# Linear attention into a two-layer expert on one core: the divided rows stored from GpSimd's queue, SyncE's transfers of a slot in another order, early fetches of late operands, weight sums loaded a period ahead

## The chip, the cores and the metric

One core of one Trainium2 chip runs the whole program. The metric is the device time of one execution in microseconds, as the median of several runs. Engines: PE (TensorE matmul), PEld (its weight loads), DVE (VectorE), ACT (ScalarE), POOL (GpSimd), SP (SyncE, which here only issues DMA transfers). SP and POOL each issue their transfers in the order of their program. An instruction that waits holds back all that stands behind it on its engine, transfers too.

## The reference

Random-feature linear attention for 8 batches and 8 heads (576 rows of 64), and then one expert (512 to 2048 to 512) with a leaky rectifier over all 4608 rows:

```python
def phi(x):
    proj = np.einsum('bhsd,df->bhsf', x, w_phi)
    proj = proj - np.max(np.abs(proj), axis=-1, keepdims=True)
    return np.concatenate([np.exp(proj), np.exp(-proj)], axis=-1)
q_p, k_p = (phi(q), phi(k))
kv = np.einsum('bhsf,bhsd->bhfd', k_p, v)
z = np.sum(k_p, axis=2)
num = np.einsum('bhsf,bhfd->bhsd', q_p, kv)
den = np.einsum('bhsf,bhf->bhs', q_p, z)[..., None] + 1e-06
attn = num / den
# x = attn as (4608, 512)
h = x @ w_in
g = np.maximum(h, 0.0) + alpha * np.minimum(h, 0.0)
out = g @ w_out
```

## The kernel before

**Attention.** The work is cut into 32 units, one for each batch and pair of heads. `places(i)` gives each step of a unit a due time, counted in slots from the unit's number, and the steps of all units are sorted by these times; so a slot holds steps of four neighbouring units. In this first part the order on PE, SP, DVE and ACT is the sorted order, and POOL's order is the scheduler's. PE projects q and k (`pj`, `pl`, L330) from `raw` (loaded at L291), DVE takes the maxima (L334) and subtracts them (L335), ACT takes exponentials, PE sums `kv` (L372, L389), then the denominators `d` (L455) and the numerators `n` (L437).

**The division** goes through DRAM to turn rows into another layout. ACT copies the denominators to `ds` (L465), SP sends 4.5 KB of them back as a tile of 128 rows of 9 (`den_out`, L469), DVE takes the reciprocal (`invert`, L474), SP writes it to `rec_d` (`rec_out`, L477) and reads it back twice as a broadcast over 64 partitions (`spread`, `rr`, L482), POOL multiplies the numerators `s` with it (`finish`, L487), and SP stores the result to `x_d` (`store`, L490). The transfers of a slot are 576 KB for `raw`, 320 for `v`, 512 for `raww`, 512 for `u_d` or `v_d`, 256 for `a_d`, twice 144 for `rr`, 288 for `x_d`, and 4.5 each for `d` and `rec_d`.

**Weights.** Once a slot a block of the weights, which arrive as pairs of 32-bit words, is decoded by the times of the table `W`: SP loads `raww` (L165), ACT, DVE (L182 to L190) and POOL (L194) put a 32-bit float together, ACT casts its high part (L133), POOL subtracts for the low part (L137), and SP stores the float to `a_d` (L214) and the two parts to `u_d` or `v_d` (L215).

**The expert** keeps each product in three matmuls (high by high, low by high, high by low). The first 512 rows are done plainly: `up2` (tile `h`, L528 to L530) and `down2` (`po`, L537 to L539), 4 products of each in an order unit of about 2.8 us. Their operands are `xr0` (the first 512 rows, 1 MB, L564), `wo` (weights of the first up products, six of 512 KB, L604) and `wd` (of the down products, 1 MB each, L597). The other 4096 rows go in four pairs of 512-row chunks by a scheme with 7 products in place of 8: eight units of up products (7 products of 6 matmuls, L803 to L805, out tiles `pa`, `pb`, `pc`), then the down products (`qa`, `qb`, `qc`) with weights `wv` that SP loads at L898.

**Sums of weights.** The 7-product scheme needs sums of weight blocks. For each of 8 up and 8 down units `sums` has five steps: `load` (POOL's queue, `a_d` to `su` or `sv`, L661), `two` (DVE, L670 and L671), `four` (DVE, L676 and L677), `high` (ACT cast, L133), and `rest` (DVE low part, L137, and two stores from POOL's queue to `us_d` or `vs_d`, L688). The table `SUMS` places the first ten of them; the other six (`v2` to `v7`) go one to a unit in the first pair's loop.

**Rows for the pairs.** `prepare(p)` loads two tiles `xr` of 1 MB each from `x_d` (POOL's queue, L743; one buffer) and makes seven operands `xo` of each on ACT (L133) and DVE (L137, L750).

In this second part the order on PE, SP and POOL is that of the program, and DVE and ACT are ordered by the scheduler. The sums of the first pair's loop live in a pool `sq` of four buffers. It is closed before the seventh unit of the pair, and the pool of `wv` takes its place, so that the first `wv` load has to wait for the last stores out of `sq`.

Of the kernel before, what the change touches and what calls it, by code (L numbers as in the profile page):

```python
# [8 lines left out]
F32 = mybir.dt.float32  # L9
# [7 lines left out]
P = 128  # L17
# [24 lines left out]
RW_BUFS = 4  # L42
# [16 lines left out]
def places(i):  # L59
    early = i < ZP  # L60
    end = i >= NPAIR - 2
    first = {}
    if i == 0:
        first = dict(
            kz=0.5093, ka=0.6934, ko=0.8124, kr=1.1197, kc=1.4241,
            n=1.8361, q=(0.96, 0.9362, 0.4904), qe=(0.9994, 1.4139, 0.8939),
        )
    if i == 1:
        first = dict(kz=0.0015, ka=0.0046, ko=0.0058)
    return dict(  # L70
        ld=-1.9685,
        lv=-0.6051,
        p=(-0.9955 if early else -0.997, -0.2197),
        pl=-0.2217,
        ke=(-0.1643, -0.0202),
        ks=(-0.0999, 0.2674, 0.4111),
        kz=0.9861,
        ka=1.0012,
        ko=1.0028,
        kr=1.0191,  # L80
        kc=1.1461,
        q=(1.4089, 1.4543, 1.3558),
        qe=(1.4364, 1.4627, 1.3892),
        d=1.9966,
        ds=2.0026,
        n=2.0062,
        s=2.1311,
        d9=2.3091,
        dv=2.7686 if early else 2.842 if end else 2.7432,
        rd=2.9461 if early else 3.1211 if end else 2.8029,  # L90
        rr=3.2683 if early else 3.3511 if end else 2.967,
        x=3.3998 if early else 3.4169 if end else 3.0674,
        xs=3.7743 if early else 3.7643 if end else 3.402,
    ) | first


W = dict(load=-0.6044, scale=-0.2534, split=-0.1196, rest=0.0025, add=0.4009, high=0.635, low=0.7532, store=0.999)
X0T = (27.2, 28.2, 28.7, 29.2, 29.7)
X0L = 0.1151
WDT = (27.5, 28.5)  # L100
WUT = (28.0, 28.4, 28.8)
HEADS = (31.9, 32.3, 32.62, 32.9)
T2 = 33.05
HEAD = 4
# [1 line left out]
U2 = 1 / 3  # L106
GQ = (0.1093, 0.2682, 0.3222)
UPA = 2
SUM0, SUMD = 2.0, 2.6
SUMS = (0.0, 0.9, 1.3, 1.7, 2.5)  # L110
NDS = 2
XP0, XPD = 8.0, 1.45


@with_exitstack
def fused_kernel(ctx: ExitStack, tc: tile.TileContext, kq, v, w_phi, w_in, w_out, alpha, out):
# [116 lines left out]
    def behind(eng):  # L233
        return tc.issue_after(newest[eng].ins)
# [49 lines left out]
    def attention_units(i):  # L284
# [202 lines left out]
            pool.tensor_tensor(c["s"], c["s"], c["r"], op=ALU.mult)  # L487

        def store():
            nc.sync.dma_start(x_d[hp, :, b * S : (b + 1) * S], c["s"])  # L490

        at = places(i)
        us = [
# [156 lines left out]
    def sums(u, down=False):  # L650
        k = "v" if down else "u"
        st = {}

        def load():
            if "sq" in late:
                tiles = [late["sq"].tile([P, 4 * WN], F32, tag="sq", name=f"s{k}_{u}_{n}", bufs=4) for n in range(3)]
            else:
                tiles = [late["s"].tile([P, 4 * WN], F32, tag="s", name=f"s{k}_{u}", bufs=3)]
                tiles += [w1t.tile([P, 4 * WN], F32, tag="wraw", name=f"sd{k}_{u}_{n}", bufs=RW_BUFS) for n in range(2)]
            a = tiles[0].rearrange("p (n c) -> p n c", n=4)  # L660
            pool.dma_start(a, a_d[int(down), u])  # L661
            a11, a12, a21, a22 = (a[:, n] for n in ((0, 2, 1, 3) if down else (A11, A12, A21, A22)))
            src = (a[:, 0:2], a[:, 2:4]) if down else (a[:, 1:3], a[:, 0:4:3])
            dst = [t.bitcast(F32R).rearrange("p (n t c) -> p n t c", t=2, c=WN) for t in tiles[1:]]
            st.update(pairs=list(zip((0, 2), src, dst)), b=(a11, a12, a21, a22))

        def two():
            a11, a12, a21, a22 = st["b"]
            with behind("dve"):
                dve.tensor_tensor(a22, a21, a22, op=ALU.add)  # L670
                dve.tensor_tensor(a21, a11, a21, op=ALU.subtract)  # L671

        def four():
            a11, a12, a21, a22 = st["b"]
            with behind("dve"):
                dve.tensor_tensor(a11, a22, a11, op=ALU.subtract)  # L676
                dve.tensor_tensor(a12, a12, a11, op=ALU.subtract)  # L677

        def high():
            with behind("act"):  # L680
                for n, a, t in st["pairs"]:
                    rnd(act, t[:, :, 0], a)

        def rest():
            for n, a, t in st["pairs"]:
                with behind("dve"):
                    low(dve, t[:, :, 1], a, t[:, :, 0])
                pool.dma_start((us_d, vs_d)[down][u, :, n : n + 2], f(t))  # L688

        return load, two, four, high, rest  # L690
# [98 lines left out]
        for dt, g in zip(SUMS, parts):  # L789
            todo.append((t1 + (SUM0 + SUMD * n + dt) * U2 + 0.002, g))  # L790
    for n in range(16):
        todo.append((t1 + (XP0 + XPD * n) * U2 + 0.003, lambda n=n: (prep.extend(prepare(1) if n == 0 else []), pieces(1))))
    end = t1 + (len(order) - HEAD) * U2 - 0.002
    todo.append((end, lambda: load_up(1, 0)))
    todo.append((end + 10, turn_on))
# [178 lines left out]
    with tc.manual_schedule(engines={et.PE, et.SP, et.Pool}):  # L974
# [10 lines left out]
        for p in range(1, NC2 // 2 + 1):  # L985
            more_pairs = p < NC2 // 2
            queue += [(p, k, u) for k in range(len(ORDER)) for u in range(NU)]
            for u in range(NU):
                if p == 1 and u == NU - 2:
                    sq.close()  # L990
                    late["wv"] = ctx.enter_context(tc.tile_pool(name="wvp", bufs=4, reuse_waits="tile"))
                if u == UX and more_pairs:
                    prep += prepare(p + 1)
                    pieces(1)
                if u == NU - 1:
                    for h in range(3):
                        load_wv(p, 0, h)
                if p == 1 and u == 0:
                    vs = [sums(n, True) for n in range(NDS, NU)]
                    vs[0][0]()  # L1000
                if p == 1 and u < len(vs):
                    for g in vs[u][1:]:
                        g()
                    if u + 1 < len(vs):
                        vs[u + 1][0]()
                if u or p > 1:
                    ahead[1]()
                if u + 1 < NU:
                    load_up(p, u + 1)
                if u == 0 and p == 1:  # L1010
                    for h in held:
                        give(*h)
                ahead[2]()
                now, ahead = ahead, unit(p, u + 1) if u + 1 < NU else None
                if ahead:
                    ahead[0]()
                else:
                    for _ in range(NLAST):
                        next(downs)
                now[3]()  # L1020
                if u < NH - 1:
                    some_operand()
                if u == NU - 2:
                    downs = down_pair(p)
            some_operand()
            if more_pairs:
                load_up(p + 1, 0)
                ahead = unit(p + 1, 0)
            for n, _ in enumerate(downs):
                if more_pairs and n == len(ORDER) * NU * 2 - NLAST - NNEXT:  # L1030
                    ahead[0]()
# [39 lines left out]
```

## Time and profile before

| what | value |
|---|---|
| median of 3 runs | 1160.08 us (1158.88, 1160.08, 1166.88) |
| the profiled execution's own time, and its span | 1160.64 us, 1158.8 us |
| PE busy | 1064.1 us, 92% of the span |
| PEld, DVE, ACT busy | 824.5, 751.7, 615.4 us |
| POOL busy | 176.5 us |
| moved by DMA | 270.11 MB, mean 233 GB/s |
| chain that ended last | PE 76%, DMA 10%, issue 8%, DVE 3%, POOL 2% |

Times in the rows are microseconds from the start of the span. In a row of the timeline the first number is the start, the second the duration, then engine, line, operation and `out<-in`; square brackets hold the idle time of the engine just before, and what ended it. Attention runs from about 20 to 385 us, the first 512 rows to 457 us, and the four pairs from there to the end.

### The profile page before, as it was taken

The numbers are of one execution on the slowest core, as the hardware profiler recorded it, in microseconds if no ns is written. First come the engines' busy times: TensorE is split into PE (matmuls) and PEld (weight loads), VectorE is DVE, ScalarE is ACT, GpSimd is POOL, SyncE is SP. The second block draws the span as 40 slices with busy tenths as digits, with TensorE's granted clock in tenths as the row PEclk, the third lists the DMA queues.
The fourth block names the chain that finished last, engine by engine and source line by source line (L and its number), as shares of the span: only waits on it lengthen the run. The fifth ranks groups of instructions, "written<-read, shape, count | busy, mean of one in ns | idle before, by whom it ended". The sixth has DMA issues, their size and how long they took to land.

```text
span 1158.8 us, 19845 instructions
## 1 busy us (share of the span) xinstructions
PE 1064.1 (92%) x7601; PEld 824.5 (71%) x7601; DVE 751.7 (65%) x1205; ACT 615.4 (53%) x1164; POOL 176.5 (15%) x192
## 2 busy tenths in 40 slices
PE   9999999999879998299609999999999999999998
PEld 6676666667556786278408888888788887888887
DVE  7868777677654345558628665588745696555764
ACT  5777777677556323245405554465544565444553
POOL 1334333333323210111110010000100001000000
PEclk9999999999999999599859999999999999999999
DMA  5888897887995697587657766566755757555465
GB/s 186 267 254 266 249 268 244 258 267 251 303 319 166 187 358 295 200 294 273 241 183 243 240 208 215 191 237 198 265 208 191 245 181 254 191 189 194 161 205 177
DMA packets 107582, 270.11 MB, mean 233 GB/s; under 512 B 18848, under 2 KB 19488, under 8 KB 106464
## 3 DMA queue, kind: packets, MB, share of 16 engines
q1 hardware_dynamic: 95632, 227.09, 60.1%
q0 software_dynamic: 11568, 41.69, 9.9%
q8 instruction: 60, 0.98, 0.3%
q14 instruction: 34, 0.28, 0.1%
q10 hardware_dynamic: 288, 0.07, 0.0%
HBM read 207.69 MB, written 60.96 MB: 232 GB/s over the span
## 4 chain that ended last, share of the span: by engine, by line
PE 76%; DMA 10%; issue 8%; DVE 3%; POOL 2%; ACT 1%; SPq 1%; ACTq 0%; POOLq 0%; DVEq 0%
PE kv L372 5%; PE n L437 5%; PE pa L803 5%; PE pa L804 5%; PE pa L805 5%; PE pj L330 5%; PE qa L803 4%; PE qa L804 4%; PE qa L805 4%; PE kv L389 3%; PE qc L803 3%; PE qc L805 3%; PE qc L804 3%; PE pc L805 2%; PE pc L804 2%
## 5 line engine op out<-in xcount | busy, mean ns | idle before, releaser
L137 DVE TENSOR_TENSOR hv<-g,hv 128x512 fp32r<-128x512 f32 x224 | 152.5, 689 | 79.1 <-ACT hv L133 78.9
L133 ACT CAST hv<-g 128x512 fp32r<-128x512 f32 x224 | 138.6, 622 | 122.0 <-DVE hv L137 55.3
L803 PE MATMUL qa<-hv,wv 128*128 128x512 f32 (+1 forms) x257 | 100.7, 392 | 39.1 <-DMA wv<-v_d 39.1
L804 PE MATMUL qa<-hv,wv 128*128 128x512 f32 (+1 forms) x257 | 100.5, 391 | 0.0
L805 PE MATMUL qa<-hv,wv 128*128 128x512 f32 (+1 forms) x257 | 100.2, 390 | 0.0
L707 POOL DMA_DIRECT2D out_dram<-pt x31 | 17.0, 547 | 531.8 <-ACT pt L970 443.6
L330 PE MATMUL pj<-w_sb,raw 64*128 64x128 f32 x1024 | 74.2, 285 | 17.8 <-issue 12.5
L330 PEld LDWEIGHTS pj<-w_sb,raw 64*128 64x128 f32 x1024 | 65.0, 193 | 30.9 <-issue 22.3
L334 DVE TENSOR_REDUCE m<-pj 128x8 f32<-128x1024 f32 (+2 forms) x67 | 78.4, 1170 | 9.1 <-PE pj L330 9.0
L803 PEld LDWEIGHTS qa<-hv,wv 128*128 128x128 f32 x257 | 48.6, 189 | 49.9 <-DMA wv<-v_d 39.6
L335 DVE TENSOR_TENSOR t<-pj,m 128x1024 f32<-128x1024 f32 (+2 forms) x67 | 78.9, 1177 | 4.8 <-ACT s L448 0.5
L437 PE MATMUL n<-qf,sf 128*64 128x288 f32 x512 | 72.3, 427 | 0.0
L487 POOL TENSOR_TENSOR s<-s,rr 128x576 f32<-128x576 f32 x32 | 45.5, 1422 | 151.8 <-DMA rr<-rec_d 142.0
L349 ACT ACTIVATE xk<-t 128x1024 f32<-128x1024 f32 (+1 forms) x66 | 64.3, 1028 | 4.7 <-DVE t L335 4.7
L428 ACT ACTIVATE qf<-qt 128x512 f32<-128x512 f32 x128 | 66.8, 633 | 0.0
L823 ACT ACTIVATE r<-g 128x512 f32<-128x512 f32 x65 | 37.6, 624 | 50.7 <-DVE g L819 50.7
L372 PE MATMUL kv<-xk,v 128*64 128x256 f32 x512 | 62.3, 385 | 0.0
L824 DVE SCALAR_TENSOR_TENSOR g<-r,al,g 128x512 f32<-128x512 f32 x65 | 46.2, 748 | 18.1 <-ACT r L823 18.1
L474 DVE RECIPROCAL r<-d 128x9 f32<-128x9 f32 x32 | 6.9, 215 | 76.6 <-DMA d<-ds 76.6
L194 POOL TENSOR_TENSOR aw<-ew,aw 128x512 f32<-128x512 f32 x32 | 40.7, 1273 | 101.4 <-DVE ew L190 101.4
L805 PEld LDWEIGHTS qa<-hv,wv 128*128 128x128 f32 x257 | 48.7, 189 | 10.2
L804 PEld LDWEIGHTS qa<-hv,wv 128*128 128x128 f32 x257 | 48.7, 189 | 10.1
(177 smaller groups left out, 2568.3 us busy)
## 6 DMA issues: line engine op xcount, KB each, us to landing
ws<-us_d SPq DMA_DIRECT2D x64, 512.0 KB
wv<-vs_d SPq DMA_DIRECT2D x64, 512.0 KB, 4.3
wv<-v_d SPq DMA_DIRECT2D x48, 512.0 KB, 5.0
wa<-u_d SPq DMA_DIRECT2D x37, 512.0 KB
raw<-kq_dram SPq DMA_DIRECT2D x31, 576.0 KB, 6.0
v<-v_dram SPq DMA_DIRECT2D x32, 320.0 KB, 7.2
rr<-rec_d SPq DMA_DIRECT2D x64, 144.0 KB, 5.8
x_d<-s SPq DMA_DIRECT2D x32, 288.0 KB, 2.3
```

The source lines that it names most:

```text
L133: return act.copy(dst, src)
L137: return eng.tensor_tensor(dst, src, f(hi), op=ALU.subtract)
L330: pe.matmul(dst[h, j], lhsT=c["raw"][hs, ts], rhs=w_sb[hs], start=True, stop=True)
L334: dve.tensor_reduce(m, src, axis=AX.X, op=ALU.max, apply_absolute_value=True)
L335: dve.tensor_tensor(t[:, hs, js], src, m.unsqueeze(3).broadcast_to([P, nh, nj, FD]), op=ALU.subtract)
L349: act.activation(x[:, a, :, js], c["t", 0][:, :, js], AF.Exp, scale=sg)
L372: pe.matmul(c["kv"][h * D : (h + 1) * D, 0:2], lhsT=c["v"][:, tp, h, :], rhs=c["x", ch][:, :, h, j, :], start=tp == 0, stop=tp == NV - 1,)
L428: act.activation(c["qf"][:, h, a, : 4 * P], ps.rearrange("p j f -> p (j f)"), AF.Exp, scale=sg)
L437: pe.matmul(ps[h * D : (h + 1) * D, :], lhsT=c["st"][:, a, h * D : (h + 1) * D], rhs=c["qf"][:, h, a, u * HS : (u + 1) * HS], start=a == 0 ...
L803: pe.matmul(ps, lhsT=wh, rhs=xh, start=first, stop=False, skip_group_check=True)
L804: pe.matmul(ps, lhsT=wl, rhs=xh, start=False, stop=False, skip_group_check=True)
L805: pe.matmul(ps, lhsT=wh, rhs=xl, start=False, stop=end, skip_group_check=True)
```

## The change

The store of the divided rows (`store`) goes from SP's queue to POOL's, where it follows `finish`. The due times of SP's steps in a slot are moved, so that its nine transfers of a slot come in another order. `xr0` is fetched 8 slots earlier, the two `wd` tiles 12.3 and 10.3 slots, the three pairs of `wo` 15.8, 7.2 and 4.6 slots, and the first `xr` of the first pair goes from the stage of the first 512 rows to slot 24.5 of attention. `sums` takes its output tiles in `high` and no longer in `load`, `SUMS` puts `load` 3.0 order units ahead of `two`, and in the first pair's loop the next `load` stands before the stores of the sum at hand. No arithmetic is added or taken out. From L653 on the line numbers rise by 1 to 3 (L661 becomes L662, L688 L690, L743 L745, L819 L822).

```diff
@@ places
-        ld=-1.9685,
-        lv=-0.6051,
+        ld=-1.65,
+        lv=-0.45,
...
-        d9=2.3091,
+        d9=2.025,
...
-        rd=2.9461 if early else 3.1211 if end else 2.8029,
-        rr=3.2683 if early else 3.3511 if end else 2.967,
+        rd=2.82,
+        rr=3.03,
...
-W = dict(load=-0.6044, ..., store=0.999)
-X0T = (27.2, 28.2, 28.7, 29.2, 29.7)
+W = dict(load=-0.83, ..., store=0.9)
+X0T = (19.2, 20.2, 21.2, 22.2, 23.2)
...
-WDT = (27.5, 28.5)
-WUT = (28.0, 28.4, 28.8)
+WDT = (15.2, 18.2)
+WUT = (12.2, 21.2, 24.2)
...
-SUM0, SUMD = 2.0, 2.6
-SUMS = (0.0, 0.9, 1.3, 1.7, 2.5)
+SUM0, SUMD = 3.1, 2.6
+SUMS = (-3.0, 0.0, 0.2, 0.6, 1.0)
...
-XP0, XPD = 8.0, 1.45
+XP0, XPD = 8.0, 1.35
...
         def store():
-            nc.sync.dma_start(x_d[hp, :, b * S : (b + 1) * S], c["s"])
+            pool.dma_start(x_d[hp, :, b * S : (b + 1) * S], c["s"])
...
         def high():
+            dst = [st["new"](n + 1).bitcast(F32R).rearrange("p (n t c) -> p n t c", t=2, c=WN) for n in range(2)]
+            st["pairs"] = list(zip((0, 2), st["src"], dst))
...
     for n in range(16):
-        todo.append((t1 + (XP0 + XPD * n) * U2 + 0.003, lambda n=n: (prep.extend(prepare(1) if n == 0 else []), pieces(1))))
+        t = t1 + (XP0 + XPD * n) * U2 + 0.003 if n else 24.5
+        todo.append((t, lambda n=n: (prep.extend(prepare(1) if n == 0 else []), pieces(1))))
...
                 if p == 1 and u < len(vs):
-                    for g in vs[u][1:]:
+                    for n, g in enumerate(vs[u][1:]):
                         g()
-                    if u + 1 < len(vs):
-                        vs[u + 1][0]()
+                        if n == 2 and u + 1 < len(vs):
+                            vs[u + 1][0]()
```

In `sums.load` the lines that took three tiles now take one, and leave a function `st["new"]` for the other two; up sums now take all three names from one counter (`su_1`, `su_2` in place of `sdu_0`, `sdu_1`).

SP in one slot of attention, before (`s` divided rows, `r` reciprocals, `aw` a decoded float, `raww` its raw words or two parts, `ds` denominators):

```order
L490 DMA x_d<-s_2575 128x576
L477 DMA rec_d<-r_15_2767 128x9
L214 DMA a_d<-aw_0_0_2612 128x512
L215 DMA u_d<-raww_0_0_2585 128x1024
L291 DMA raw_2877<-kq_dram 128x1152
L482 DMA rr_2884<-rec_d 64x576 x2
L469 DMA d_16_2887<-ds_2846 128x1x9
L165 DMA raww_1_0_2889<-w_out_dram 128x1024
L295 DMA v_2898<-v_dram 128x640
```

And in the changed kernel, in the slot that also holds the early `xr0`:

```order
L469 DMA d_17_3037<-ds_3006 128x1x9
L482 DMA rr_3039<-rec_d 64x576 x2
L165 DMA raww_1_0_3042<-w_out_dram 128x1024
L564 DMA xr_3049<-x_d 128x4x512
L291 DMA raw_3051<-kq_dram 128x1152
L295 DMA v_3075<-v_dram 128x640
L477 DMA rec_d<-r_17_3081 128x9
L214 DMA a_d<-aw_1_0_2924 128x512
L215 DMA v_d<-raww_1_0_2888 128x1024
```

The store of `s` is gone from the row, `d` comes first, and `raw` comes behind the broadcast reads and the weight load instead of ahead of them.

POOL's queue at the second `xr` of the first pair (`su` the floats of an up sum, `sdu` or `su_1`, `su_2` its two output tiles), before:

```order
L661 DMA su_5520<-a_d 128x1024
L688 DMA us_d<-sdu_0_5521 128x1024
L688 DMA us_d<-sdu_1_5522 128x1024
L661 DMA su_5583<-a_d 128x1024
L743 DMA xr_1_5630<-x_d 128x2x1024
L688 DMA us_d<-sdu_0_5584 128x1024
```

And in the changed kernel:

```order
L690 DMA us_d<-su_1_5500 128x1024
L690 DMA us_d<-su_2_5501 128x1024
L662 DMA su_5528<-a_d 128x1024
L690 DMA us_d<-su_1_5559 128x1024
L690 DMA us_d<-su_2_5560 128x1024
L662 DMA su_5606<-a_d 128x1024
L745 DMA xr_1_5610<-x_d 128x2x1024
L690 DMA us_d<-su_1_5630 128x1024
```

Before, a load is followed by the stores of the same sum; now a load stands ahead of the stores of the sum before it. In both, `xr_1` comes behind the stores of the sixth sum.

DVE at the end of the up units of the first pair, where `g_7_11` takes PE's last product ahead of the down products (`pa_7`); before:

```order
L137 TENSOR_TENSOR sv_1_5988<-sv_0_5987,sv_1_5988 128x2x256
L819 TENSOR_TENSOR g_7_11_6526<-pa_7_6480,p_1_7_6545 128x512
L137 TENSOR_TENSOR sv_2_5989<-sv_0_5987,sv_2_5989 128x2x256
L137 TENSOR_TENSOR xo_2_0_6732<-xr_0_6069,xo_2_0_6732 128x512
L137 TENSOR_TENSOR xo_3_0_6809<-xr_0_6069,xo_3_0_6809 128x512
...
L137 TENSOR_TENSOR sv_2_6083<-sv_0_6081,sv_2_6083 128x2x256
...
L137 TENSOR_TENSOR sv_2_6175<-sv_0_6173,sv_2_6175 128x2x256
...
L137 TENSOR_TENSOR sv_2_6267<-sv_0_6265,sv_2_6267 128x2x256
```

And in the changed kernel:

```order
L137 TENSOR_TENSOR sv_2_6258<-sv_0_6169,sv_2_6258 128x2x256
L822 TENSOR_TENSOR g_7_11_6526<-pa_7_6480,p_1_7_6545 128x512
L137 TENSOR_TENSOR xo_4_0_6886<-xr_0_6067,xo_4_0_6886 128x512
L670 TENSOR_TENSOR sv_0_6261<-sv_0_6261 128x256
L671 TENSOR_TENSOR sv_0_6261<-sv_0_6261 128x256
L676 TENSOR_TENSOR sv_0_6261<-sv_0_6261 128x256
L677 TENSOR_TENSOR sv_0_6261<-sv_0_6261 128x256
L137 TENSOR_TENSOR sv_1_6347<-sv_0_6261,sv_1_6347 128x2x256
L137 TENSOR_TENSOR sv_2_6348<-sv_0_6261,sv_2_6348 128x2x256
```

Before, three whole sums (`v5`, `v6`, `v7`) stand behind `g_7_11`; now only the last.

## Rows read from the trace of the kernel before

**Rows 1.** The waits of PE, longest first: line, what it waited for, us in total, times, longest.

```profile
PE qa L803 <- DMA wv<-v_d: 39.1, 1, 39.1
PE pa L803 <- ACT xo L133: 26.5, 1, 26.5
PE pj L330 <- issue: 12.5, 5, 3.7
```

**Rows 2.** PE's timeline: the first `kv` row of a slot, the first and the last of 29 (34.82 and 354.42), two neighbours (264.02 and 274.59), and one slot with its first `pj` (140.94 to 154.94).

```profile
34.82 1.95 PE L372 MATMUL kv<-xk,v 128*64 128x256 f32 x16
...
140.94 1.95 PE L372 MATMUL kv<-xk,v 128*64 128x256 f32 x16
...
145.03 1.16 PE L330 MATMUL pj<-w_sb,raw 64*128 64x128 f32 x16 [1.72 <-issue]
...
154.94 1.95 PE L372 MATMUL kv<-xk,v 128*64 128x256 f32 x16
...
264.02 1.95 PE L372 MATMUL kv<-xk,v 128*64 128x256 f32 x16
...
274.59 0.65 PE L372 MATMUL kv<-xk,v 128*64 128x256 f32 x4
...
354.42 1.95 PE L372 MATMUL kv<-xk,v 128*64 128x256 f32 x16
```

**Rows 3.** The waits views of SP's queue, of POOL and of DVE, one row of each, in the same columns as rows 1.

```profile
SPq L490 <- POOL s L487: 146.9, 32, 6.4
...
POOL s L487 <- DMA rr<-rec_d: 142.0, 30, 11.1
...
DVE r L474 <- DMA d<-ds: 76.6, 30, 5.4
```

**Rows 4.** The timelines of ACT, DVE, POOL and SP over the slot from 262.5 to 275, an engine at a time.

```profile
266.51 0.39 ACT L465 ACTIVATE ds<-d 128x288 f32<-128x288 f32 x1
...
273.19 0.22 DVE L474 RECIPROCAL r<-d 128x9 f32<-128x9 f32 x1 [2.94 <-DMA d<-ds]
...
262.46 1.42 POOL L487 TENSOR_TENSOR s<-s,rr 128x576 f32<-128x576 f32 x1 [3.87 <-DMA rr<-rec_d]
263.84 1.29 POOL L137 TENSOR_TENSOR raww<-aw,raww 128x512 fp32r<-128x512 f32 x1
...
273.87 1.42 POOL L487 TENSOR_TENSOR s<-s,rr 128x576 f32<-128x576 f32 x1 [4.72 <-DMA rr<-rec_d]
...
263.91 0.33 SPq L490 DMA_DIRECT2D x_d<-s  x1
...
265.31 0.39 SPq L215 DMA_DIRECT2D v_d<-raww  x1
265.80 0.41 SPq L291 DMA_DIRECT2D raw<-kq_dram  x1
266.54 1.18 SPq L482 DMA_DIRECT2D rr<-rec_d  x2
267.81 0.58 SPq L469 DMA_DIRECT2D d<-ds  x1
```

**Rows 5.** Two landing times: the last line of the view of L291 (the `raw` loads), from issue to landing; and the last broadcast reads of attention on SP's timeline, when little else was in flight.

```profile
DMA to landing us min/median/max: 4.3/5.8/7.9
...
398.60 1.10 SPq L482 DMA_DIRECT2D rr<-rec_d  x2
```

**Rows 6.** A table of stretches: from, to, length, then busy time and instructions of PE, PEld, DVE, ACT and POOL, granted clock, DMA share, GB/s.

```profile
197.00:300.00 103.00, 98.73 (x1301) 69.29 (x1295) 76.09 (x126) 73.95 (x157) 37.99 (x29) 1.00 0.82 258
300.00:360.00 60.00, 48.95 (x592) 34.21 (x590) 37.12 (x59) 36.28 (x82) 15.68 (x12) 0.94 0.90 303
```

**Rows 7.** POOL's timeline in the stage of the first 512 rows: the last `finish`, the first sum's stores, the second `xr`.

```profile
402.39 1.67 POOL L487 TENSOR_TENSOR s<-s,rr 128x576 f32<-128x576 f32 x1 [10.27 <-DMA rr<-rec_d]
404.02 1.13 POOL L688 DMA_DIRECT2D us_d<-sdu  x2
...
475.56 0.71 POOL L743 DMA_DIRECT2D xr<-x_d  x1
```

**Rows 8.** PE's timeline around its first long stop: the last up product's last matmul, the first matmul after the stop; and the view of L743 (`xr`), its last line.

```profile
454.49 0.40 PE L530 MATMUL h<-x0pt,ws 128*128 128x512 f32 x1
...
484.88 0.79 PE L803 MATMUL pa<-xo,wa 128*128 128x512 f32 x1 [26.52 <-ACT xo L133]
...
DMA to landing us min/median/max: 5.8/8.9/11.5
```

**Rows 9.** The end of PE's second long stop, on the timelines of DVE, POOL, SP and PE in turn: the eviction of the last up product, the last sum's first operation, its stores, the first `wv` load, the first down product.

```profile
569.66 0.68 DVE L819 TENSOR_TENSOR g<-pa,p 128x512 f32<-128x512 f32 x1
...
596.60 0.42 DVE L670 TENSOR_TENSOR sv<-sv 128x256 f32<-128x256 f32 x1 [6.11 <-DMA sv<-a_d]
...
599.66 1.14 POOL L688 DMA_DIRECT2D vs_d<-sv  x2 [7.81 <-DVE sv L137]
...
602.77 2.75 SPq L898 DMA_DIRECT2D wv<-v_d  x4
...
607.36 0.80 PE L803 MATMUL qa<-hv,wv 128*128 128x512 f32 x1 [39.12 <-DMA wv<-v_d]
```

**Rows 10.** The views of L688 and L182, a row of each: transfers issued by POOL (nanoseconds, least, median, most), and a DVE operation on one input that runs twice a slot with L189.

```profile
L688 POOL DMA_DIRECT2D us_d<-sdu x16: 534/534/597, 404.0 to 496.0; - x16
...
L182 DVE TENSOR_SCALAR aw<-aw x32: 416/417/1301, 18.1 to 364.4; 128x512 uint32<-128x512 uint32 x32
```

More of the change, by code (lines that the diff above doesn't have):

```diff
@@ L94, in places @@
     ) | first
-W = dict(load=-0.6044, scale=-0.2534, split=-0.1196, rest=0.0025, add=0.4009, high=0.635, low=0.7532, store=0.999)
-X0T = (27.2, 28.2, 28.7, 29.2, 29.7)
+W = dict(load=-0.83, scale=-0.2534, split=-0.1196, rest=0.0025, add=0.4009, high=0.635, low=0.7532, store=0.9)
+X0T = (19.2, 20.2, 21.2, 22.2, 23.2)
 X0L = 0.1151
-WDT = (27.5, 28.5)
-WUT = (28.0, 28.4, 28.8)
+WDT = (15.2, 18.2)
+WUT = (12.2, 21.2, 24.2)
 HEADS = (31.9, 32.3, 32.62, 32.9)
@@ L655, in load @@
             if "sq" in late:
-                tiles = [late["sq"].tile([P, 4 * WN], F32, tag="sq", name=f"s{k}_{u}_{n}", bufs=4) for n in range(3)]
-            else:
-                tiles = [late["s"].tile([P, 4 * WN], F32, tag="s", name=f"s{k}_{u}", bufs=3)]
-                tiles += [w1t.tile([P, 4 * WN], F32, tag="wraw", name=f"sd{k}_{u}_{n}", bufs=RW_BUFS) for n in range(2)]
-            a = tiles[0].rearrange("p (n c) -> p n c", n=4)
+                st["new"] = lambda n: late["sq"].tile([P, 4 * WN], F32, tag="sq", name=f"s{k}_{u}_{n}", bufs=4)
+                a = st["new"](0)
+            else:
+                st["new"] = lambda n: w1t.tile([P, 4 * WN], F32, tag="wraw", name=f"s{k}_{u}_{n}", bufs=RW_BUFS)
+                a = late["s"].tile([P, 4 * WN], F32, tag="s", name=f"s{k}_{u}", bufs=3)
+            a = a.rearrange("p (n c) -> p n c", n=4)
             pool.dma_start(a, a_d[int(down), u])
@@ L663, in load @@
             src = (a[:, 0:2], a[:, 2:4]) if down else (a[:, 1:3], a[:, 0:4:3])
-            dst = [t.bitcast(F32R).rearrange("p (n t c) -> p n t c", t=2, c=WN) for t in tiles[1:]]
-            st.update(pairs=list(zip((0, 2), src, dst)), b=(a11, a12, a21, a22))
+            st.update(src=src, b=(a11, a12, a21, a22))
         def two():
```

## The prediction

> **What bounds the kernel now.** PE is busy for 92% of the span, so its idle time is what a change of order can give back. The list of PE's waits comes first [rows 1]: two single stops, 39.1 us (the first down weights `wv`) and 26.5 us (an operand `xo` of the first pair), and small waits of `pj` that come to 12.5 us under "issue". The rest is spread over attention, and is read off PE's timeline [rows 2]: a slot in which nothing is late takes 274.59 − 264.02 = 10.57 us, but the 28 slots from 34.82 to 354.42 take 319.60 us, 23.5 us more than 28 x 10.575. One slot shows how: 140.94 to 154.94 is 14.0 us, 3.43 too long, though its `pj` waits only 1.72. The matmuls behind it run slower too.
>
> What makes a slot late is a ring through SP's queue. SP waits 146.9 us for POOL's `s`, POOL 142.0 us for `rr`, and DVE's reciprocal 76.6 us for `d` [rows 3]; none of the three engines is short of time. In one slot [rows 4] POOL multiplies at 262.46, SP can store only at 263.91, and only behind that store do `rr` (266.54) and `d` (267.81) go out. `rr` lands so that the next `s` starts at 273.87: a round of 11.41 us, against 10.575 for PE's slot. `d` is 4.5 KB, its source is written at 266.90, yet it is issued at 267.81 and the reciprocal starts only at 273.19, 4.8 us after the issue ended at 268.39. DVE takes its program in order, so the maxima for the next projection stand behind the reciprocal.
>
> **The sum is made against 1160.64 us**, the profiled execution's own time, 0.05% above the median of 1160.08 us.
>
> **Store on POOL, SP's order.** Nothing is added: 32 stores change the engine that issues them. The ring now runs over `s` 1.42, the store's issue on POOL 0.53 (as L688, [rows 10]), the low part that stands behind it on POOL 1.29, the `u_d` or `v_d` store that waits for this 0.39, `d` 0.58, `rr` 1.18, and some 0.2 between them: 5.6 us, and then the landing of `rr`. Its bounds are 2.7 us after the end of the issue with little in flight (399.70 [rows 5] to 402.39 [rows 7]) and 6.15 with `a_d`, `v_d` and `raw` (1.37 MB) ahead (267.72 to 273.87 [rows 4]). `raw` no longer goes ahead, so between 0.5 and 0.8 MB are left there, and in proportion the landing is 4.0 to 4.7. The round is then 9.6 to 10.3 us (bounds 8.3 and 11.75), under the slot. For `d` the due times tell the margin: from its issue to the reciprocal it was 2.7432 − 2.3091 = 0.434 slots, 4.6 us, less than it takes; now 0.718 slots, 7.6 us, 2.8 more than it takes. The DVE waits should go, and with them the 23.5 us.
>
> What is late next is `raw`. From its issue to the first projection the due times leave 0.653 slots, 6.9 us, where there were 0.972 (10.3). It lands after 5.8 us in the median and 7.9 at most [rows 5], which holds in a plain slot.
>
> **Early fetches.** They take 7 MB (two `wd`, three pairs of `wo`, `xr0`, the first pair's `xr`) into six slots that had nothing of the kind. At the 303 GB/s of the stretch where these now lie [rows 6] one MB is 3.5 us, and most of them are issued right ahead of a `raw`: it then lands after 9.3 us, 2.4 too late. Between nothing (the slots before run ahead) and 2.4 I take 1.3, in six slots 8 us. In return the slots from 300 to 360, where PE now stands for 60.00 − 48.95 = 11 us, have the plain load of the others, 258 in place of 303 GB/s [rows 6]. Attention then loses 8 us where it lost 23.5: **−15.5** (bounds: −23.5 when every `raw` holds, and no gain).
>
> **Sums a period ahead, up side.** The 26.5 us are the wait for the second `xr`. POOL issues it at 475.56, behind the stores of the sixth sum, whose round is load, land, four additions, casts, stores, and only then the next load; the first sum is stored at 404.02 [rows 7], so a sum took 14 us. Now the load is due 3 order units (8 us) before the additions, so its landing is out of the round; what remains is some 3 us of DVE and ACT work (596.60 to 599.66 in a like sum, [rows 9]) and two issues of 0.53 [rows 10], and the plan's 2.6 units of 2.8 us, 7.3 us, rules. Five more sums from 404.02 end at 440, `xr` is issued by 442 and lands 8.9 us later (11.5 at most) [rows 8], at 451 to 453. In the changed order its first operand stands on DVE behind the last up product's, whose matmul starts at 454.49 [rows 8]: about 457. PE wants it at 484.88 − 26.52 = 458.4. So the stop closes, with 1 us left for what doesn't fit: **−25.5**. The cover is the cadence of the sums: past 8.1 us each (442 + 5 x 0.9 + 8.9 = 455.4) every 0.1 us more costs 0.5. With 10 us each, 10 us of the stop stay.
>
> **Sums a period ahead, down side.** The 39.1 us run from 568.24 to 607.36. PE waits for `wv`, this for the pool of the sums to close, this for the stores of the last sum `v7`. From the last sum's first operation to PE it is 607.36 − 596.60 = 10.76 us [rows 9]: additions and casts 3, stores' issue and landing 3, `wv` 4.6. Before, three sums stand behind `g_7_11` on DVE, which takes PE's last product (569.66), and each waits for its own load. In the changed order one stands there, and its load is long in. Then PE starts again 0.3 (the eviction's start) + 1.3 (two operations of 0.69 or less) + 10.76 = 12.4 us after it stopped; I take 12.5: **−26.6** (bounds: 10.8 left when `v7` isn't held by `g_7_11`, 21.5 when the sum before it is late too, by as much again).
>
> **Sum:** 1160.64 − 15.5 − 25.5 − 26.6 = 1093.0. The clock behind each stop would give about a microsecond more, which I leave out.
>
> **A rule against the change.** DMA transfers that POOL issues took 534 to 597 ns on 16 stores, with DVE at work most of the time, and DVE's one-input operation, of which a slot has two, takes 0.42 us, once 1.30 [rows 10]. Nothing there holds a POOL issue by more than 0.06 us. The Trainium skill ("SBUF — State Buffer", "A bandwidth-pool intuition that's wrong (but worth ruling out)") says that a transfer issued by GpSimd took about 3100 ns in place of 620 beside a DVE copy, since its descriptors wait for the port that DVE holds. By the rows the sum stays as it is; by that page's figure each store would be 2.48 us later in the ring, and the time, as an estimate from it, 1139 us. The rows do not bear the rule out so far, though none of them is of a store inside attention.
>
> **Rivals.**
> 1. *The ring stays the bound.* `rr` lands as late as before (6.15), the round is 11.75. For it: the `u_d` store now stands in the ring with POOL's low part. Against: `raw` is out of the way. From a landing of 5.0 us on the ring is slower than PE. With attention as it was the time is 1093 + 15.5 = 1108; with 1.18 over in 31 slots (36.4 in place of 23.5), 1121.
> 2. *The last sum isn't earlier.* DVE's order is the scheduler's, made by its own costs; if the loads of `v5` to `v7` or their buffers (four, of which a sum takes three) come free late, the stop stays 39: 1093 + 26.6 = 1120. For it: the low parts of a sum must be stored before the second next one takes their buffers. Against: each sum now has a whole up unit of PE, 42 matmuls, for a few us of work.
> 3. *POOL's stores are held* in attention. A hold of s us makes the round 9.6 + s, over PE's slot from s = 1.0 on. A hold as long as the two DVE operations of a slot (0.84) would cost nothing. Two operations as long as the longest seen (1.30, [rows 10]) would hold it 2.6 us: (9.6 + 2.6 − 10.575) x 31 = 50, 1143.
> 4. *Slower: `raw` is late in every slot.* Its margin shrinks by 3.4 us to 6.9, and 7.9 was seen. If PE waits in each slot and runs its next matmuls slower, as from 140.94 to 154.94 [rows 2], a slot costs 3.43 us: 28 x 3.43 = 96 in place of 23.5, 1093 + 15.5 + 72.5 = 1181. It decides from some 22 such slots on. Against: the median leaves 1.1 us, and less traffic stands ahead of `raw`.
> 5. *The change doesn't do what it says*: both stops stay and attention gains little, 1145 to 1160.
>
> **How the numbers follow.** The forecast has 0.58; its own range, from its bounds (attention −23.5, both stops at their least; on the other side a stop that is 10 longer), is 1081 to 1105. Rival 1 has 0.17, rival 2 0.11, rival 3 0.04, rival 4 0.05, rival 5 0.05. A range from 1080 to 1121 holds the forecast and the first two, 0.86 in all, less what falls outside of their ends. About 1% (12 us) is what a measurement of this kernel can tell from no change. Faster by more than that are the forecast, rivals 1 to 3 and a part of 5, 0.92; within it 0.03; slower 0.05.
>
> **What would show it.** Right: PE's list of waits without 26.5, and 12 to 13 us in place of 39.1; the reciprocal's wait for `d` down from 76.6 to under 15; neighbouring `kv` rows 10.6 apart but for six slots; POOL's store issues at 0.53. Wrong: `s` waiting for `rr` with slots of 11 us or more (rival 1); `vs_d` stores some 30 us behind PE's stop (rival 2); POOL's stores of 1.5 us or more (rival 3); `pj` or its weight loads waiting for `raw` in slot after slot, with a granted clock below 0.95 (rival 4).

## The result: 1110.2 us, and where the time went

The changed kernel takes 1110.22 us (median of 4 runs, 1108.46 to 1116.75), the kernel before 1159.48 (4 runs): a ratio of 0.9582, 95% interval 0.9529 to 0.9634. In two of the experiments below one of the four executions took two or three times as long as the others (run 3: 3652.41 us; run 8: 2134.82 us, the profiled one), and their medians are those of the other three. By the medians the change saves 49.3 us. The profiled execution is the slowest of the four, 1116.75 us with a span of 1114.9; its span is 43.9 us shorter than that of before. PE's list of waits in the changed kernel (line, what it waited for, us in total, times, longest):

```profile
PE pj L330 <- DMA raw<-kq_dram: 15.8, 6, 3.7
PE qa L806 <- DMA wv<-v_d: 12.2, 1, 12.2
PE pa L806 <- ACT xo L133: 4.0, 1, 4.0
PE pa L806 <- DMA wa<-u_d: 3.7, 2, 2.6
```

Against [rows 1], the stop for `wv` has gone from 39.1 to 12.2 and that for `xo` from 26.5 to 4.0. In the place of 12.5 under "issue" stand six waits for `raw`. The waits of DVE, SP and POOL that made the ring of [rows 3]:

```profile
DVE r L474 <- DMA d<-ds: 5.4, 3, 3.1
...
SPq L215 <- POOL raww L137: 103.0, 31, 5.5
...
SPq L482 <- DMA rec_d<-r: 22.6, 7, 7.3
...
POOL s L487 <- DMA rr<-rec_d: 124.8, 32, 11.9
```

The reciprocal hardly waits for `d` any more (5.4 us, before 76.6). SP no longer waits for `s` (146.9 us before), but 103.0 for the low part of a weight block, which stands behind `s` on POOL. The first `kv` rows of the slots, as in [rows 2], run from 34.62 to 353.37 in 28 slots:

```profile
34.62 1.95 PE L372 MATMUL kv<-xk,v 128*64 128x256 f32 x16
...
353.37 1.95 PE L372 MATMUL kv<-xk,v 128*64 128x256 f32 x16
```

That is 318.75 us, 22.65 more than 28 x 10.575; before it was 23.5. The account of the profiled executions, from the times of these rows and of the first down product (384.11, was 385.11): attention and what lies ahead of it −1.0; the first 512 rows +0.8; the stop for `xo` −22.5; the first pair's up units +5.1 (below); the stop for `wv` −26.9; the rest +0.6. Sum −43.9.

Six slots are late, those from 140.52, 177.85, 213.43, 226.64, 250.36 and 284.42, by 5.6, 3.9, 2.6, 2.6, 2.3 and 5.5 us. The first and costliest of them on SP, POOL and PE in turn (start, duration, engine, line; idle time before in brackets), and below it PE's first matmuls in the fourth:

```profile
133.87 1.11 SPq L482 DMA_DIRECT2D rr<-rec_d  x2
135.03 0.58 SPq L165 DMA_DIRECT2D raww<-w_in_dram  x1
135.65 0.91 SPq L604 DMA_DIRECT2D wo<-u_d  x2
136.65 0.38 SPq L291 DMA_DIRECT2D raw<-kq_dram  x1
137.07 0.61 SPq L295 DMA_DIRECT2D v<-v_dram  x1
137.78 0.44 SPq L477 DMA_DIRECT2D rec_d<-r  x1
...
143.22 0.59 SPq L469 DMA_DIRECT2D d<-ds  x1
147.22 1.11 SPq L482 DMA_DIRECT2D rr<-rec_d  x2
...
127.96 1.43 POOL L487 TENSOR_TENSOR s<-s,rr 128x576 f32<-128x576 f32 x1 [3.49 <-DMA rr<-rec_d]
...
137.42 1.42 POOL L487 TENSOR_TENSOR s<-s,rr 128x576 f32<-128x576 f32 x1 [2.20 <-DMA rr<-rec_d]
139.14 0.58 POOL L490 DMA_DIRECT2D x_d<-s  x1 [0.30 <-POOL s L487]
...
151.34 1.41 POOL L487 TENSOR_TENSOR s<-s,rr 128x576 f32<-128x576 f32 x1 [6.59 <-DMA rr<-rec_d]
...
140.52 1.95 PE L372 MATMUL kv<-xk,v 128*64 128x256 f32 x16
142.30 0.60 PE L372 MATMUL kv<-k,v 128*64 128x256 f32 x4
145.43 2.08 PE L330 MATMUL pj<-w_sb,raw 64*128 64x128 f32 x16 [2.53 <-DMA raw<-kq_dram]
147.44 4.11 PE L437 MATMUL n<-qf,sf 128*64 128x288 f32 x16
...
156.70 1.51 PE L372 MATMUL kv<-xk,v 128*64 128x256 f32 x12
...
231.52 1.16 PE L330 MATMUL pj<-w_sb,raw 64*128 64x128 f32 x16 [2.50 <-DMA raw<-kq_dram]
232.61 2.16 PE L437 MATMUL n<-qf,sf 128*64 128x288 f32 x16
```

Ahead of `wo` the ring goes round in 137.42 − 127.96 = 9.46 us, and `rr` lands 2.4 us behind its issue. The 1 MB of `wo` at 135.65 makes late whatever is issued behind it: `raw` lands 8.4 us after its issue ended (137.03 to 145.43), and the next `rr`, which reads what is written to `rec_d` from 137.78 on, goes out only at 147.22 (SP waits for that write in seven slots, 22.6 us in all). The next round is 13.92 us, the slot 16.18. PE waits 2.53 in it, and loses another 3 because the matmuls behind the wait run slow (`n` takes 4.11, one slot earlier 2.16). Their granted clock is 0.50, the lower level (1.2 GHz); a row of the table of stretches (from, to, length, busy time of PE, PEld, DVE, ACT, POOL, granted clock, DMA share, GB/s):

```profile
145.43:151.47 6.04, 6.04 (x32) 3.49 (x32) 2.57 (x3) 0.40 (x1) 0.13 (x1) 0.50 0.70 214
```

This isn't so behind every wait: in the slot from 226.64 PE waits 2.50, `n` takes 2.16 as ever, and the slot is late by little more than the wait. Slow matmuls follow three of the six waits, and they make up most of the 6.9 us by which the 22.65 exceed the 15.8 of waiting.

### The profile page after: what moved, and what is told of

Its sections match the earlier page's. It is cut to its first block, busy times and chain, and to the rows that moved or that the text cites. A ratio compares the mean times of both kernels' runs of the same rounds, so it can differ in the third digit from the quotient of the medians.

```text
span 1114.9 us, 19887 instructions
## 1 busy us (share of the span) xinstructions
PE 1067.5 (96%) x7601; PEld 825.6 (74%) x7601; DVE 754.5 (68%) x1205; ACT 615.3 (55%) x1164; POOL 196.9 (18%) x224
## 3 DMA queue, kind: packets, MB, share of 16 engines
q0 software_dynamic: 14128, 51.13, 12.3%
## 4 chain that ended last, share of the span: by engine, by line
PE 47%; issue 32%; DMA 13%; DVE 5%; ACT 1%; POOL 1%; SPq 0%; ACTq 0%; POOLq 0%; DVEq 0%
PE n L437 6%; DMA raw<-kq_dram 5%; PE pj L330 5%; PE kv L372 5%; DMA xr<-x_d 3%; PE kv L389 3%; PE pa L806 2%; PE pa L808 2%; PE pa L807 2%; PE d L455 2%; DMA su<-a_d 2%; DMA wa<-u_d 2%; PE qt L418 2%; PE qa L807 2%; PE qa L806 2%
## 5 line engine op out<-in xcount | busy, mean ns | idle before, releaser
L806 PE MATMUL qa<-hv,wv 128*128 128x512 f32 (+1 forms) x257 | 100.9, 393 | 12.2 <-DMA wv<-v_d 12.2
L330 PE MATMUL pj<-w_sb,raw 64*128 64x128 f32 x1024 | 73.6, 284 | 18.4 <-DMA raw<-kq_dram 15.8
L448 ACT COPY s<-n 128x288 f32<-128x288 f32 x64 | 25.5, 400 | 78.7 <-PE n L437 75.1
```

Source lines behind the costliest of these rows:

```text
L330: pe.matmul(dst[h, j], lhsT=c["raw"][hs, ts], rhs=w_sb[hs], start=True, stop=True)
L806: pe.matmul(ps, lhsT=wh, rhs=xh, start=first, stop=False, skip_group_check=True)
```

## The experiments

Each was run beside the kernel before on the same chip. "Lost in attention" is, as above, the time between the first `kv` rows of 28 slots less 28 x 10.575 (before 23.5, changed 22.65), in the profiled execution. The profiled execution lies 6.5 us above the median for the changed kernel and 5.2 below it in run 1; so differences of a few us between two kernels' lost times are not shown by these numbers.

**1. Early fetches behind `raw` and `v`** (`fetch_behind`)

```diff
-X0T = (19.2, ...), WDT = (15.2, 18.2), WUT = (12.2, 21.2, 24.2)
+X0T = (18.6, ...), WDT = (15.6, 17.6), WUT = (12.6, 20.6, 23.6)
```

> The changed kernel with its early fetches moved behind raw and v in a slot (wo at 12.6, 20.6 and 23.6 slots, wd at 15.6 and 17.6, xr0 at 18.6); raw keeps its due time, so its margin of 0.653 slots stays. Theory A (a raw is late only because a fetch of 1 MB is issued right ahead of it): the six waits of pj for raw, 15.8 us, go, neighbouring kv rows are 10.58 apart but for the slot of the first pair's xr, and the time falls from 1110 to 1090 to 1096. Rival B (the shorter margin alone makes raw late): 1108 to 1112, as many waits. Rival C (a slot cannot move a MB more in 10.6 us, wherever it stands): something else is late in the same slots, 1104 or more.

1109.52 us (1104.37 to 1118.29), ratio 0.9579, 0.9517 to 0.9641; lost in attention 15.9. `pj`'s waits for `raw` fell to 7.7 us, but new ones came:

```profile
PE pj L330 <- DMA raw<-kq_dram: 7.7, 6, 2.9
PE pa L806 <- DMA wa<-u_d: 7.2, 3, 3.0
PE qt L415 <- ACT s L448: 6.3, 6, 1.7
```

Theory A is not enough, C came nearer. B's time fits too, and so does its number of waits, but they are half as long, and run 3 is against it. PE waits for ACT, and ACT for a buffer of `s` that its store hasn't left: the MB now stands ahead of `rec_d`, and so of `rr`.

**2. `raw` ahead of the early fetches** (`raw_first`)

```diff
-        ld=-1.65,
+        ld=-1.85,
```

> The changed kernel with raw due at -1.85 slots in place of -1.65: it goes ahead of the early fetches, and has 0.853 slots to land in place of 0.653. Theory A (fetch ahead of raw) and rival B (margin too short) both say that the waits for raw go: 1088 to 1096. Rival C (bytes of a slot) says that little is won: 1104 or more.

1106.84 us (1105.93 to 1113.98), ratio 0.9544, 0.9494 to 0.9593; lost in attention 14.5, with 6.0 us of waits for `raw` in eight pieces and 6.0 for `s`. Again less than A and B say.

**3. The slot order alone** (`slot_only`): `SUMS`, `XPD`, the loop and the fetch times as before.

> Only the order of a slot is changed: the store on POOL, SP's order and margins as in the changed kernel; the fetches and the sums as in the kernel before. Theory A: no pj waits for raw up to 295 us, DVE's reciprocal waits under 10 us in all, slots of 10.58; the late fetches still cost some 10 to 14 us between 295 and 365; both long stops stay; 1147 to 1153. Rival B (margin too short): waits for raw in plain slots too, 1155 to 1162.

1143.56 us (1142.53 to 1146.11), ratio 0.9851, 0.9800 to 0.9902: faster, by 1 to 2%. No slot up to 299 us is late: two rows of the table of stretches:

```profile
30.00:299.00 269.00, 268.09 (x3603) 189.82 (x3601) 213.16 (x334) 202.90 (x432) 115.39 (x102) 1.00 0.81 270
299.00:360.00 61.00, 49.85 (x587) 33.78 (x581) 35.18 (x53) 34.59 (x76) 20.12 (x18) 0.97 0.80 285
```

PE stands for 0.9 us in 269. So the order and the store do all that the prediction said of them, and the shorter margin of `raw` costs nothing in a plain slot, against rival B. The late fetches then cost 12.6 us in the last slots. The time is below what was expected; its two stops are 22.2 and 31.3 there.

**4. The sums alone** (`sums_only`): slot order, store and fetches as before.

> Only the sums are changed (loads a period ahead, output tiles taken in high, the times of the second xr 1.35 units apart); slot order, store and fetches as in the kernel before. If the two stops close by the sums alone: 26.5 becomes 2 to 6, 39.1 becomes 11 to 14, the up units of the first pair run 3 to 5 us longer, 1111 to 1118. Rival: the first stop needs the first xr to be fetched in attention as well, and 10 us or more of it stay: 1120 to 1130.

1121.58 us (1116.77 to 1123.36), ratio 0.9651, 0.9605 to 0.9697. The stops are 9.2 and 15.1 us. The rival was nearer, by its time and almost by its stop. With the first `xr` in that stage the second is issued at 446.96 and lands after 17.6 us (445.96 and 15.5 in the changed kernel).

**5. Early fetches put back** (`no_early`): the slot order and the sums, fetches as before.

> The changed kernel with the early fetches put back to the times of the kernel before (the slot order, the store on POOL and the sums stay changed). If the early fetches give nothing as they stand, since they cost in slots 12 to 25 what they save in the last three: 1103 to 1111, with slots of 10.58 up to 299 us and 12 to 14 us lost behind that. Rival: they are needed for the first long stop to close (the first xr), the stop stays at 8 us or more and the time is 1114 to 1122.

1111.50 us (1109.82 to 1113.13), ratio 0.9580, 0.9551 to 0.9608, the same as the changed kernel within these intervals, and just above the first range. The slots are 10.58 up to 299 us and then 11.57, 16.36 and 18.38: 14.8 us are lost in attention where the changed kernel loses 22.65, but the two stops keep 9.1 and 14.2, 5 and 2 us more; a first stop of over 8 us is what the rival said. As they stand, the early fetches give nothing in the whole that can be told from the spread.

**6. The store back on SP** (`store_sp`)

```diff
-            pool.dma_start(x_d[hp, :, b * S : (b + 1) * S], c["s"])
+            nc.sync.dma_start(x_d[hp, :, b * S : (b + 1) * S], c["s"])
```

> The changed kernel with the store of the divided rows back on SP's queue, where its due time puts it behind v and ahead of the reciprocal's store. Theory E (SP's order did it: rr goes out half a slot ahead of that store, so s is ready when SP comes to it): 1106 to 1114, SP's wait for s under 30 us. Rival (the ring through SP's queue closes again): slots of 11 us and more, SP's wait for s over 100 us, 1125 to 1140.

1114.06 us (1112.15 to 1115.77), ratio 0.9601, 0.9572 to 0.9631, which overlaps with the changed kernel's. SP waits for `s` again, but the ring stays open: up to 139.89 us, and from 302.77 to 355.65, every slot is 10.58. Between these lie the early fetches, and 25.4 us are lost in attention:

```profile
SPq L490 <- POOL s L487: 78.3, 31, 3.9
SPq L215 <- POOL raww L137: 21.1, 17, 3.8
```

The two waits together are 99 us, about the 103 of the changed kernel: SP waits for POOL at one place or the other. Theory E misses on the wait (under 30 was said) and is 0.06 us over its range with the time, far below the rival's. So it is the order of SP's transfers that opened the ring; which of the moves in it did, no run takes apart. The queue of the store is worth 3.8 us by the medians, which the intervals don't tell from nothing. The Trainium skill ("DMA: Bandwidth & Descriptors", "Issuing engines are not separate DMA queues") says that issuing from another engine saves only the sequencer's time, and this run agrees as far as its interval goes.

**7. A third `raw` buffer** (`raw3`)

```diff
-RAW_BUFS = 2
+RAW_BUFS = 3
-        ld=-1.65,
+        ld=-2.65 if i > 2 else -1.65,
```

> The changed kernel with three buffers for raw and each raw issued a whole slot earlier (due at -2.65, at the same place in SP's order of a slot, from the fourth unit on), so that raw can no longer be late; the early fetches stay ahead of it, 1 MB in one slot. If raw's margin is all that the early fetches hurt: no wait for raw, attention loses 5 us or less in place of 22.6, 1090 to 1097. Rival (the bytes are paid for in the ring instead, since rr and the stores of s come late when a slot carries a MB more): waits of ACT for the buffers of s take their place, about 2 us a MB, 14 us lost, 1100 to 1107.

1106.13 us (1105.35 to 1107.34), ratio 0.9527, 0.9496 to 0.9558; lost in attention 16.3. The waits for `raw` are gone and those for `s` stand in their place:

```profile
PE qa L806 <- DMA wv<-v_d: 12.6, 1, 12.6
PE qt L415 <- ACT s L448: 10.3, 8, 2.8
PE pa L806 <- DMA wa<-u_d: 4.1, 2, 3.1
```

The rival held, at its size. A late `raw` is only the first thing that a MB more in a slot makes late; the ring pays next.

**8. The early fetches in halves** (`halves`)

```diff
-WDT = (15.2, 18.2)
-WUT = (12.2, 21.2, 24.2)
+WDT = ((13.6, 14.6), (19.6, 20.6))
+WUT = ((11.6, 12.6), (15.6, 16.6), (21.6, 22.6))
...
-X0T = (19.2, 20.2, 21.2, 22.2, 23.2)
+X0T = (17.6, 20.2, 21.2, 22.2, 23.2)   # second half at 18.6
...
+    todo.append((25.5, lambda: held_x.pop()()))   # second half of the first pair's xr
```

> The changed kernel with the 7 MB of early fetches cut into 14 transfers of 512 KB, one to a slot and behind raw and v (slots 11.6 to 22.6, the first pair's xr at 24.5 and 25.5). Theory C (a plain slot has room for about half a MB more in its 10.6 us, not for a whole one): slots of 10.58 to 10.9, pj's waits for raw and the waits for the buffers of s under 3 us in all, the 22.6 us that attention still loses in the changed kernel fall under 7, 1094 to 1100. Rival D (each MB costs its 2 us wherever it stands, since the ring has no room at all): 1104 to 1112.

1097.95 us (1097.81 to 1100.23), ratio 0.9469, 0.9437 to 0.9501. The time is in theory C's range and under rival D's. What C says of slots and waits can't be read here, but in run 9, which has the same fetches.

**9. Halves, and the second `xr` one sum earlier** (`halves_xpd`)

```diff
-XP0, XPD = 8.0, 1.35
+XP0, XPD = 8.0, 1.1
```

> The early fetches in halves, one to a slot, and the pieces of the first pair 1.1 order units apart. The two parts are apart in time, so they add: attention as with the halves (slots of 10.58 to 10.9, less than 7 us lost in it), no wait of more than 1 us for the second xr, the stop for wv at 12 to 13: 1094 to 1099. Rival: what the second xr gains is lost in the up units of the first pair, whose loads of wa then come late: 1097 to 1101.

1093.71 us (1089.94 to 1098.61), ratio 0.9442, 0.9378 to 0.9506: faster than before and than the changed kernel, whose interval begins at 0.9529. The time is 0.3 us under the first range. Lost in attention 7.0, as said; but its slots reach 12.37 us where 10.9 was the most, so theory C's price is right and its picture of the single slot is not. Its waits of PE, and the stretch that holds the early fetches, here and in the changed kernel:

```profile
PE qa L822 <- DMA wv<-v_d: 12.3, 1, 12.3
PE qt L415 <- ACT s L448: 3.8, 5, 1.6
PE pa L822 <- DMA wa<-u_d: 3.4, 2, 2.0
...
140.00:299.00 159.00, 153.93 (x2026) 107.59 (x2020) 127.04 (x192) 115.80 (x249) 66.68 (x59) 1.00 0.91 303
```

```profile
140.00:299.00 159.00, 143.24 (x1817) 99.99 (x1813) 110.33 (x173) 104.32 (x225) 60.24 (x53) 0.96 0.84 281
```

In these 159 us 303 in place of 281 GB/s go through, PE stands for 5.1 in place of 15.8 us, and its granted clock is 1.00, the upper level (2.4 GHz), in place of 0.96. Against run 1, whose whole MBs stand behind `raw` and `v` as well, the lost time falls from 15.9 to 7.0 and the time from 1109.5 to 1093.7; the slots of the fetches and the second `xr`'s place differ too.

**10. The second `xr` one sum earlier alone** (`xpd`): experiment 9's edit on the changed kernel.

> The changed kernel with the pieces of the first pair 1.1 order units apart in place of 1.35, so that POOL issues the second xr behind the stores of the fifth sum, not the sixth, some 5 us earlier. If the 4.0 us that are left of the first stop are the landing of this xr: 0 to 1 us left, and 1104 to 1109. Rival: the landing grows by as much, since the queues are full there (336 GB/s over the stage), and the time stays at 1108 to 1113.

1111.19 us (1110.72 to 1111.93), ratio 0.9577, 0.9546 to 0.9608. The wait for `xo` is gone from PE's list, yet the time is the same. In this execution attention lost 21.1 us and the waits for `wa` were 4.4, so 4 us less in one place do not show in the whole. The wait is the first theory's: `xr` is issued at 439.01 in place of 445.96, and no `xr` of this kernel lands later than 12.2 us after its issue (15.5 in the changed one), where the rival had the landing grow. The time is the rival's. The profiled executions differ by 5.2 us (1116.75 and 1111.59), the medians don't, so where the gain goes is open.

**11. Other buffers for the last sum** (`halves_rot`): two tiles of `sq` taken and dropped ahead of the first sum, on top of 9.

> As halves_xpd, with the four buffers of the sums in the first pair's loop used from another one on (two tiles taken and dropped ahead of the first sum), so that the last sum ends in other buffers than the first wv takes. If the first wv load waits for its own piece of the pool alone, it goes out before PE stops and PE has work of 2.8 us more, and the stop of 12 us falls to 7 to 10: 1091 to 1096. Rival (each wv overlaps several of the buffers, or only the last stores count): 12 us as before, 1094 to 1101.

1094.48 us (1090.28 to 1099.77), ratio 0.9441, 0.9385 to 0.9496. The stop is 10.6 in place of 12.3 us, and the time is that of 9, in both ranges. The mechanism is not the rival's: the first `wv` load goes out at 535.25, ahead of the last sum's stores (535.61), where in run 9 it followed them (535.62 and 532.46). But it still goes out 5.3 us after PE stopped (8.3 in run 9). One execution each, and stops of 12.2 to 15.1 in the other kernels with these sums, don't show that the 1.7 us are a gain.

**12. A dose of bytes** (`dose`): `no_early` with `wd` fetched over and over.

```diff
+    def again(n):
+        nc.sync.dma_start(f(wd[0])[:, :n], v_d[0, :, :n])
+    for n in range(6):
+        todo.append((6.6 + n, lambda: again(2)))
+    for n in range(8):
+        todo.append((14.6 + n, lambda: again(4)))
```

> One look at the price of extra bytes: the changed kernel with the early fetches put back, and with the first down weights fetched again and again behind raw and v, 512 KB in each of slots 6 to 11 and 1 MB in each of slots 14 to 21 (the first time at 5.6). Theory C (room for half a MB, not for a whole one): the slots with 512 KB stay at 10.58 to 10.8 us, those with 1 MB are 11.3 to 12.5. Rival D (every byte costs): 11.3 or more in the first group, 12.5 in the second.

1137.81 us (a single execution). The seven slots from 65.84 to 146.03 are 11.46 us in the mean, 6.2 us in all longer than plain ones, for six halves and the whole MB issued at 61.78, just ahead of them: 1.5 us for a MB. The nine from 167.23 to 281.76 are 12.73, 19.4 in all, for 8 MB: 2.4 each. Both means are rival D's, and theory C falls as it was put: a slot has no half a MB of free room. But a MB in halves costs less than a whole one. PE waits 21.2 us for ACT's copy into `s`, and ACT's wait for the store of `s` shows where it is paid:

```profile
ACT s L448 <- DMA x_d<-s: 46.9, 17, 4.3
```

In `halves_xpd` the 7 MB cost 7.0 us, 1.0 each, though its halves follow each other too, from slot 11 to 22. Why the dose costs more than that is open.

## Why the prediction was right, and where it was not

The time, 1110.2, is in the range, and faster was right; but it is not in the likeliest case's own range (1081 to 1105). The range reaches so far only for rivals 1 and 2, and the cause of neither came about, so that it holds the time is in part luck. Made against the profiled execution, the sum said −67.6 and the trace says −43.9. By its terms:

- **Store and order of the slot: right.** The round was put at 9.6 to 10.3 us and is 9.46, `d`'s wait at under 15 and it is 5.4, and without the fetches no slot up to 299 us is late (run 3). Of the two moves in this term SP's order is the one that counts (run 6). POOL's issue of a store, at 0.53 in the sum, is 0.58:

```profile
L490 POOL DMA_DIRECT2D x_d<-s x32: 547/583/707, 42.4 to 404.6; - x32
```

- **The rule that POOL's transfers wait for DVE** (the Trainium skill, "SBUF — State Buffer", "A bandwidth-pool intuition that's wrong (but worth ruling out)"): none of these 32 issues took over 0.71 us, and the 2.48 us more that the prediction estimated from that page's figure are not seen in this kernel. Rival 3 is out. It is no test of the rule itself, though: only one of the 32 issues ran beside DVE's one-input operation (L182), and it took 0.60 us:

```profile
287.34 0.42 DVE L182 TENSOR_SCALAR aw<-aw 128x512 uint32<-128x512 uint32 x1
...
287.39 0.60 POOL L490 DMA_DIRECT2D x_d<-s  x1 [0.30 <-POOL s L487]
```

- **Early fetches: the step that failed.** The prediction took 1.3 us for each of six slots, between nothing and 2.4, 8 in all, and set −15.5 for attention. The six slots are there, one by one, but cost 22.65 us, 3.8 each, and attention gained 0.9. The term's other end, "no gain", was named, but 2.4 in each of six slots, 14.4, doesn't reach it. Two things were mis-sized. `raw` was late by a little more than the upper bound of 2.4, not by half of it: PE waits 15.8 us in the six, 2.6 each. And nothing was put down for the lower clock behind such a wait, most of the other 6.9 us, though the prediction had read it from [rows 2]. A third thing it left out comes to light only when `raw` is on time: it let the ring stay at 9.6 in such a slot, where the store to `rec_d` and `rr` stand behind the MB as well and the round is 13.92. Run 7 shows it: PE never waits for `raw` there, and 16.3 us stay lost. In runs 1 and 2, where `raw` waits fell to 7.7 and 6.0, 15.9 and 14.5 do. The forecast's rival 1 gave the right time (1108), but not the cause: in plain slots the ring isn't the bound.
- **Sums, up side: right to 3 us.** 4.0 us are left where 1.0 was allowed. `xr` was issued at 445.96, where the sum said 442, and landed 15.5 us later, against the 8.9 that was taken and the 11.5 that had been seen [rows 8]; 368 GB/s moved meanwhile, at a DMA share of 1.00. The view of `xr` and that stretch:

```profile
DMA to landing us min/median/max: 5.6/9.1/15.5
```

```profile
446.00:461.50 15.50, 12.11 (x51) 9.13 (x50) 8.38 (x16) 3.87 (x8) 3.91 (x7) 1.00 1.00 368
```

- **Missing from the sum: +5.1** in the first pair's up units, from the end of one stop to the start of the next, 88.49 us (462.17 to 550.66) where it was 83.36 (484.88 to 568.24). PE waits 3.7 there for `wa`, with more traffic than before (300 GB/s, was 279):

```profile
462.17:550.66 88.49, 84.62 (x345) 66.57 (x345) 67.39 (x117) 48.63 (x87) 10.52 (x20) 0.96 0.82 300
```

```profile
484.88:568.24 83.36, 82.35 (x345) 65.65 (x345) 60.63 (x103) 43.77 (x78) 9.57 (x18) 0.98 0.80 279
```

  It is tempting to say that closing the stop brings this traffic forward. The runs don't bear that out: in run 3, with a stop of 22.2 us ahead of it and 276 GB/s, the stretch takes 89.47 us and PE never waits for `wa`; in run 4, with a stop of 9.2 and 302 GB/s, it takes 83.93. The cause is open.

```profile
469.89:559.36 89.47, 85.22 (x345) 66.80 (x345) 64.38 (x110) 46.25 (x83) 11.00 (x21) 0.96 0.78 276
```

```profile
465.21:549.14 83.93, 82.75 (x345) 65.51 (x345) 65.86 (x113) 47.85 (x84) 10.17 (x19) 0.98 0.83 302
```

- **Sums, down side: right.** 12.2 us are left where 12.5 were said, and by the way that was said: the last sum's first operation starts 1.84 us after PE stopped at 550.66 (1.6 in the sum), and PE starts again 10.39 us later (10.76).

```profile
552.50 0.42 DVE L670 TENSOR_TENSOR sv<-sv 128x256 f32<-128x256 f32 x1
...
562.89 0.79 PE L806 MATMUL qa<-hv,wv 128*128 128x512 f32 x1 [12.23 <-DMA wv<-v_d]
```

The parts don't quite add: against the kernel before in their own comparisons, the slot order alone gives 17.6 us (1161.20 to 1143.56), the sums alone 39.6 (to 1121.58), both together (run 5) 50.0 (1161.51 to 1111.50). Run 3 holds a part of both: its stops are 12 us shorter in all (22.2 and 31.3) with the sums as before. Why the order of the slot shortens them isn't shown.

## What to carry to other kernels

In this kernel a transfer that was fetched early was paid for by what was issued behind it, first the next operand and then the small ones: look for the chain of 4 KB stores and reads that stands behind it, and give that chain's round, not only the operand's margin, the landing time with the extra bytes ahead. Cut such fetches and spread them over slots: in single executions whole MBs ahead of `raw` cost this kernel 3.2 us each (22.65 for 7 MB) and gave back about as much, behind it 2.3 (run 1), halves one to a slot 1.0, and the kernel with them takes 1093.7 in place of 1110.2 us (4 us of it may be the second `xr`'s place). When moving a store to another queue, look first whether the order of the queue that it leaves would have done as well.

## What was not expected of the hardware

- A wait of 2 to 4 us of PE sometimes costs nearly twice its length, and sometimes no more than itself. In the changed kernel slow matmuls follow three of six waits: 16.18 us for a slot with a wait of 2.53, where the granted clock is 0.50 (1.2 GHz) for 6.04 us, but 13.14 for a slot with a wait of 2.50, where the 16 `n` matmuls behind it take their usual 2.16 us. What decides between the two isn't shown.
- A store of 4.5 KB issued behind 1 MB took 9.0 us to land: its issue ends at 138.22, and `rr`, which SP holds back for it, goes out at 147.22.
